# Half-chunk start, reordered loads and later filter stages in a fused layernorm, spectral filter and gated MLP kernel

## The chip, the cores and the metric

The kernel runs on one core of one Trainium2 chip. The metric is the device time of one execution in microseconds (us), lower is better. Times are medians of several executions; a "span" is the time from the first to the last instruction in the one execution that the trace shows, and it is about 2 us shorter than that execution's time. An execution that took over 1.5% more than the fastest of its kernel in its group counts as slow, and ratios leave it out.

Engine names in the profile: PE is TensorE's matmuls, PEld its weight loads, DVE is VectorE, ACT is ScalarE, POOL is GpSimd, SP is SyncE, which issues most DMAs.

## The reference

The input x has 2048 rows of 512 bf16 values. Two branches start from its layernorm, and their sum is added to x:

```
xn  = layernorm(x)                                   # over the 512 columns
A   = irfft2( rfft2(xn) * (w_r + i*w_i) )            # a filter over all rows and columns
B   = ( gelu(xn @ w_gate) * (xn @ w_up) ) @ w_down   # 512 -> 1792 -> 512
out = x + A + B
```

## The kernel before

One queue of instructions is written for each engine. TensorE runs its queue in order, so the writer decides by hand when each piece of the filter branch is put between the large matmuls of the MLP branch. The rows are cut in four chunks of 512 rows, each of four row tiles of 128. Where this text numbers rows, it means row tiles: rows 0 to 3 are chunk 0, rows 4 to 7 chunk 1. Matmuls write to the banks of PSUM, and the copy of a result out of a bank is called its eviction. For each chunk there are 14 blocks, each with a `gate` group and an `up` group (four matmuls of 512 columns each), and, one chunk later, four `down` groups. After each group stands a *hook*, a numbered place where other work may be put. There are 160 of them.

```
for b in range(4):                    # chunks
    for fc in range(NFC):             # 14 blocks
        gate(b, fc); hook(False)
        up(b, fc);   flush(); hook()
        if b > 0 and fc in (2, 5, 8, 11):
            down(b - 1, (fc - 2) // 3)      # 14 matmuls, three hooks inside
for jj in range(4):
    down(3, jj)
```

What hangs on the hooks, in the order of the data: normalisation of chunks 1 to 3 (`ln_stat`, `ln_aggr`, `ln_norm`), their transposes (`trans`), a butterfly of additions (`butter`, writes the "fold" tiles), the column transform (`unit_D`, 128-point units), the 64-point row-wise units (`unit_A`), a transposition through DRAM ("scr" written, "tv" read back), `unit_B` and the filter product, `unit_C`, a second trip through DRAM ("vp" written, the "vv" view of the arena read back), `unit_row`, `unit_E` and `unit_F`. In this document the first units after the tv reload (`unit_B`) are called column units, and A the row units. `unit_B` reads the whole of tv, so the first of them has to wait for the last reload.

```
for m in range(1, 4):
    a = 10 * (m - 1)
    ...  ln_stat at a .. a+3, ln_norm at a+6, a+7, trans at a+8, a+9, butter at a+10, a+11
for j in range(NJ):
    h = (4, 6, 8, 10, 12, 14, 17, 19, 22, 24, 27, 29, 32, 33, 34, 36)[j]
    at(h, (unit_D, j))
    if j % 2:
        at(h + 2, (unit_A, j - 1), (unit_A, j))
for i in range(0, 16, 2):
    at(47 + 3 * i, (unit_B, i), (unit_B, i + 1))
    at(52 + 3 * i, (unit_C, i), (unit_C, i + 1))
at(103, (unit_row,))
for j in range(NJ):
    at(104 + 3 * j, (unit_E, j))
    at(108 + 3 * j, (unit_F, j))
```

The start runs 24 dummy matmuls (`warm(24)`) while the first rows are loaded and normalised, then transposes the whole of chunk 0 and enters the loop:

```
warm(24)
for i in range(2): ln_stat(2*i); ln_stat(2*i + 1); ln_aggr(2*i, 2)
for i in range(2): ln_norm(2*i); ln_norm(2*i + 1)
for i in range(2):
    trans(0, (0, 1), (2*i, 2*i + 1), "dve")
    trans(0, (2, 3), (2*i, 2*i + 1), "act")
```

## Time and profile before

| | before |
|---|---|
| median of the executions of the first round | 206.12 us (205.89 to 207.45) |
| span in the trace (an execution of 207.09 us) | 205.1 us |
| TensorE busy | 190.8 us, 93% |
| first gate matmul, last eviction begins, end | 10.69, 201.37, 205.1 us |

The page's busy times, then two of its rows in 40 slices of 5.1 us each: how busy TensorE was in tenths, and the clock granted to it in tenths.

```profile
PE 190.8 (93%) x1131; PEld 93.2 (45%) x1145; DVE 112.1 (55%) x262; ACT 88.3 (43%) x157; POOL 25.9 (13%) x52
...
PE   7898989899999569999999999989999999999992
...
PEclk9999999999999957999999999999999999999999
```

TensorE is nearly always busy, and in one place, in slices 15 and 16, its clock was low. The next fence is TensorE's timeline there; columns: start, duration, engine, line of the kernel, operation, output and inputs, count, and in brackets how long the engine sat idle before and what ended it.

```profile
68.63 1.03 PE L589 MATMUL ps<-xnT,wu 128*128 128x512 f16 x4
73.51 1.07 PE L455 MATMUL ps<-tv,be 128*64 128x257 f16 x8 [3.85 <-DMA tv<-scr]
74.51 1.89 PE L576 MATMUL ps<-xnT,wg 128*128 128x512 f16 x4
76.19 1.91 PE L589 MATMUL ps<-xnT,wu 128*128 128x512 f16 x4
77.90 1.73 PE L576 MATMUL ps<-xnT,wg 128*128 128x512 f16 x4
79.47 1.03 PE L589 MATMUL ps<-xnT,wu 128*128 128x512 f16 x4
```

The first column unit (L455) waits 3.85 us for tv. Then the groups behind it take twice their time. A gate or up group starts 0.86 us after the one before it at full speed; here the starts are 1.7 us apart (74.51, 76.19, 77.90). The mean granted clock from 73.5 to 80 was 0.55. Asked in short stretches, the clock was at half from about 72.5 to 79.3.

TensorE's list of waits (total us, number of times, longest), the four lines that matter:

```profile
PE ps L455 <- DMA tv<-scr: 3.9, 1, 3.9
PE ps L366 <- DVE xn L356: 1.9, 5, 0.7
PE ps L406 <- DVE arena L392: 1.2, 2, 0.7
...
PE ps L501 <- DMA arena<-scr: 0.7, 1, 0.7
```

Besides tv there are waits for normalised rows (xn), for the butterfly (fold tiles, which lie in the arena) and, in front of `unit_row` (L501), for the second reload.

The start, timeline of all engines, chosen lines. L338 is the dummy matmuls, L356 normalises, L366 transposes, L344 takes statistics, L576 is gate.

```profile
1.19 6.84 PE L338 MATMUL ps<-dumm 128*128 128x512 f16 x24 [1.19 <-DVE dumm L309]
...
7.50 0.73 DVE L356 TENSOR_SCALAR xn<-x_sb,ag,rstd 128x512 f16<-128x512 bf16 x2
...
8.38 0.61 PE L366 MATMUL ps<-ident,xn 128*128 128x128 f16 x8 [0.35 <-DVE xn L356]
...
10.61 0.69 DVE L344 BATCH_NORM_STATS2 st<-x_sb 128x6 f32<-128x512 bf16 x1 [0.46 <-DMA x_sb<-in_A_x_dram]
...
10.69 1.02 PE L576 MATMUL ps<-xnT,wg 128*128 128x512 f16 x4 [0.78 <-ACT xnT L378]
...
14.14 1.03 PE L576 MATMUL ps<-xnT,wg 128*128 128x512 f16 x4
...
20.01 0.62 PE L366 MATMUL ps<-ident,xn 128*128 128x128 f16 x8 [0.73 <-DVE xn L356]
```

The 24 dummy matmuls end at 8.03. The first two rows are normalised at 8.23, the transposes follow, and gate begins at 10.69. The gate of the third block (which the change's half blocks lead up to) begins at 14.14.

The tail, same columns:

```profile
195.12 6.21 PE L602 MATMUL ps<-wd,hT 128*128 128x512 bf16 x27
...
201.37 0.69 DVE L615 TENSOR_TENSOR osb<-ps,x_sb 128x512 bf16<-128x512 f32 x1 [2.33 <-PE ps L602]
```

One eviction of 512 columns at 201.37, then the stores, and the end of the span at 205.1: 3.7 us from the start of that eviction.

### The profile page before, as it was taken

Reading aid. Unit: us, or ns where it says so; the run is one execution under the profiler, and the core shown is the slowest. Engines: PE = TensorE matmul, PEld = TensorE weight load, DVE = VectorE, ACT = ScalarE, POOL = GpSimd, SP = SyncE. Lnnn points to the kernel's source line nnn. Section 1 sums busy time; section 2 is a strip of 40 time slices with the busy share of each in tenths; the row PEclk is TensorE's granted clock in tenths of the full one; section 3 lists DMA queues with packets and bytes.
Section 4 is the critical chain, followed back from the end, with each engine's and each line's share of the span. In section 5 each row is a group of like instructions: output and inputs, shape, how many; then the busy total and the mean of one; then the engine's idle time right before and its main releaser. Section 6 shows DMA issues by size and latency. Waiting matters only on the chain.

```text
span 205.1 us, 3107 instructions
## 1 busy us (share of the span) xinstructions
PE 190.8 (93%) x1131; PEld 93.2 (45%) x1145; DVE 112.1 (55%) x262; ACT 88.3 (43%) x157; POOL 25.9 (13%) x52
## 2 busy tenths in 40 slices
PE   7898989899999569999999999989999999999992
PEld 3344544445544223444444444435555555555540
DVE  2897786978422233546773677233555454546341
ACT  2135565554553131563545534414636363635210
POOL 0201125031201202222310000000100001010000
PEclk9999999999999957999999999999999999999999
DMA  5999998626675601556654223230011111111102
GB/s 147 221 312 348 281 316 185 197 79 150 107 180 148 120 18 54 113 131 134 157 162 118 62 77 106 69 87 1 16 46 44 36 33 50 39 27 29 26 26 51
DMA packets 19007, 23.09 MB, mean 113 GB/s; under 512 B 2208, under 2 KB 16672, under 8 KB 18608
## 3 DMA queue, kind: packets, MB, share of 16 engines
q1 hardware_dynamic: 16512, 16.79, 30.4%
q0 software_dynamic: 1712, 5.32, 11.8%
q10 hardware_dynamic: 768, 0.79, 1.6%
q8 instruction: 9, 0.15, 0.3%
q14 instruction: 6, 0.05, 0.1%
HBM read 16.57 MB, written 6.31 MB: 112 GB/s over the span
## 4 chain that ended last, share of the span: by engine, by line
PE 73%; DMA 10%; DVE 10%; issue 2%; POOL 1%; ACT 1%; SPq 0%
PE ps L602 20%; PE ps L589 20%; PE ps L576 19%; DMA tv<-scr 3%; DVE hT L592 3%; DVE st L344 3%; PE ps L455 2%; PE ps L481 2%; DMA scr<-tt 2%; DMA scr<-vp 2%; PE ps L515 2%; DMA x_sb<-in_A_x_dram 2%; DMA arena<-scr 2%; DVE xn L356 2%; PE ps L366 1%
## 5 line engine op out<-in xcount | busy, mean ns | idle before, releaser
L592 DVE TENSOR_TENSOR hT<-ps,gl 128x512 bf16<-128x512 f32 x56 | 38.5, 690 | 41.8 <-PE ps L589 36.8
L576 PE MATMUL ps<-xnT,wg 128*128 128x512 f16 x224 | 59.2, 388 | 0.8 <-ACT xnT L378 0.8
L589 PE MATMUL ps<-xnT,wu 128*128 128x512 f16 x224 | 58.4, 384 | 0.0
L579 ACT ACTIVATE gl<-ps 128x512 bf16<-128x512 f32 x56 | 33.4, 597 | 48.1 <-PE ps L576 44.9
L602 PE MATMUL ps<-wd,hT 128*128 128x512 bf16 x210 | 49.8, 379 | 0.8 <-issue 0.2
L576 PEld LDWEIGHTS ps<-xnT,wg 128*128 128x128 bf16 x224 | 21.0, 99 | 24.5 <-issue 4.8
L602 PEld LDWEIGHTS ps<-wd,hT 128*128 128x128 bf16 x224 | 21.3, 98 | 23.2 <-issue 1.0
L589 PEld LDWEIGHTS ps<-xnT,wu 128*128 128x128 bf16 x224 | 21.3, 99 | 22.2 <-issue 2.6
L523 POOL COPY zt<-xn 1x128 bf16<-1x128 bf16 x16 | 4.5, 283 | 79.4 <-ACT zt L522 79.4
L615 DVE TENSOR_TENSOR x_sb<-ps,x_sb 128x512 bf16<-128x512 f32 x11 | 7.6, 690 | 12.0 <-PE ps L602 12.0
L522 ACT ACTIVATE zt<-ps 128x512 bf16<-128x512 f32 x16 | 9.5, 595 | 10.5 <-PE ps L515 10.5
L549 ACT ACTIVATE eo<-ps 128x512 bf16<-128x512 f32 x16 | 9.5, 595 | 9.4 <-PE ps L544 9.4
L487 ACT ACTIVATE vp<-ps 128x514 bf16<-128x514 f32 x16 | 8.7, 598 | 10.1 <-PE ps L481 10.1
L344 DVE BATCH_NORM_STATS2 st<-x_sb 128x6 f32<-128x512 bf16 x16 | 10.6, 685 | 3.6 <-DMA x_sb<-in_A_x_dram 3.6
L413 ACT ACTIVATE xs<-ps 128x512 f16<-128x512 f32 x16 | 9.5, 596 | 6.7 <-PE ps L409 6.6
L461 ACT ACTIVATE xc<-ps 128x514 f16<-128x514 f32 x16 | 8.7, 600 | 6.9 <-PE ps L455 6.9
L440 ACT ACTIVATE tt<-ps 128x514 f16<-128x514 f32 x16 | 8.7, 598 | 3.7 <-PE ps L434 3.1
L554 DVE TENSOR_TENSOR ys<-eo 128x256 bf16<-128x256 bf16 x16 | 4.6, 289 | 9.3 <-ACT eo L549 9.3
L455 PE MATMUL ps<-tv,be 128*64 128x257 f16 x64 | 5.5, 297 | 3.9 <-DMA tv<-scr 3.9
L467 DVE TENSOR_TENSOR m_0<-xc,Wr 128x514 bf16<-128x514 f16 x8 | 3.4, 430 | 10.3 <-ACT xc L461 10.3
L352 POOL TENSOR_TENSOR rstd<-vpe,mhalf 128x4 f32<-128x4 f32 (+1 forms) x5 | 4.6, 918 | 26.6 <-DVE vpe L351 26.6
L338 PE MATMUL ps<-dumm 128*128 128x512 f16 x24 | 6.8, 454 | 1.2 <-DVE dumm L309 1.2
(65 smaller groups left out, 167.2 us busy)
## 6 DMA issues: line engine op xcount, KB each, us to landing
scr<-tt SPq DMA_DIRECT2D x16, 128.5 KB
tv<-scr SPq DMA_DIRECT2D x16, 128.5 KB
scr<-vp SPq DMA_DIRECT2D x16, 128.5 KB
arena<-scr SPq DMA_DIRECT2D x16, 128.5 KB
out_dram<-osb SPq DMA_DIRECT2D x32, 64.0 KB
wg<-in_B_w_gate_dram SPq DMA_DIRECT2D x3, 512.0 KB, 11.2
wu<-in_B_w_up_dram SPq DMA_DIRECT2D x3, 512.0 KB, 13.0
x_sb<-in_A_x_dram SPq DMA_DIRECT2D x5, 256.0 KB, 11.4
```

The source lines that it names most:

```text
L344: op("dve", lambda e: e.bn_stats(st[:, j, :], x_sb[:, j, :]), r=[("x", j, 0), ("x", j, 1)], w=[("st", j)])
L413: op("act", lambda e: e.activation(x4[:].rearrange("p (a c r) -> p a c r", a=2, r=4), bank(bk).rearrange("p (a r c) -> p a c r", a=2, r=4) ...
L440: op("act", lambda e: e.activation(t4[:], pair(bk), ACT.Copy, scale=SC_A), r=[("ps", bk), ("ps", bk + 1)], w=[("tt", j % 4)])
L455: ins = e.matmul(bank(bk + ri)[64 * hh:64 * hh + 64, 0:257], be[:, 64 * ri:64 * ri + 64], tv[:, 16 * hh + h, :], start=True, stop=True, sk ...
L461: op("act", lambda e: e.activation(xc[s2][:, :, 0:KD], pair(bk), ACT.Copy, scale=SC_B), r=[("ps", bk), ("ps", bk + 1)], w=[("xc", s2)])
L522: op("act", lambda e: e.activation(z[:], bank(bk).rearrange("p (a c) -> p a c", a=4), ACT.Copy, scale=SC_E), r=[("ps", bk)], w=[zk])
L549: op("act", lambda e: e.activation(o2[:], bank(bk), ACT.Copy), r=[("ps", bk)], w=[ok])
L576: ins = e.matmul(bank(bg), wg_sb[:, dc, fc * P:(fc + 1) * P], xnT[:, dc, b * 512:(b + 1) * 512], start=(dc == 0), stop=(dc == 3))
L579: op("act", lambda e: e.activation(gl[k % 2][:], bank(bg), ACT.Gelu_apprx_tanh), r=[("ps", bg)], w=[("gl", k % 2)])
L589: ins = e.matmul(bank(bu), wu_sb[:, dc, fc * P:(fc + 1) * P], xnT[:, dc, b * 512:(b + 1) * 512], start=(dc == 0), stop=(dc == 3))
L592: op("dve", lambda e: e.tensor_tensor(hT[b % 2][:, fc, :], bank(bu), gl[k % 2][:], ALU.mult), r=[("ps", bu), ("gl", k % 2)], w=[("hT", b % ...
L602: ins = e.matmul(bank(bk), hT[b % 2][:, fc, jj * P:(jj + 1) * P], wd_sb[:, fc, :], start=(fc == 0), stop=(fc == NFC - 1))
```

## The change

Its intent: (1) begin the first two MLP blocks on the first half of chunk 0, before its second half is normalised; (2) load the weights of blocks 2 to 5 ahead of rows 4 to 7 and spread them over two queues; (3) give normalisation, transposes and butterfly more distance from one another; (4) put the column units far enough behind the row units that tv is back in time, and move the rest behind them; (5) halve the last down by columns, so that eviction and store of its first half overlap with the second. There is also a third gelu buffer, two z buffers fewer, and a better model of when PSUM banks come free. The core of the diff:

```diff
-        for b, eng in ((0, "sp"), (1, "act")):
-            load_x(4, 4, b, eng)
+        load_w(wg_sb, wgv, "wg", 2, 6, "act")
+        load_w(wu_sb, wuv, "wu", 2, 6, "sp")
+        load_x(4, 4, 0, "sp")
+        load_x(4, 4, 1, "sp")
         dma("sp", fd[:], c_fd.ap(), w=["fd"])
-        load_w(wg_sb, wgv, "wg", 2, 6, "sp")
-        load_w(wu_sb, wuv, "wu", 2, 6, "sp")
...   later loads reordered in the same way
-            a = 10 * (m - 1)
+            a = 9 * (m - 1) + 3
...   ln_norm at a+5 (was a+6), trans at a+9 (was a+8), butter at a+11 (was a+10),
...   butter of chunk 0 at 3 and 4 (was 0 and 1), late loads of the filter two hooks later
-            h = (4, 6, 8, 10, 12, 14, 17, 19, 22, 24, 27, 29, 32, 33, 34, 36)[j]
+            h = (9, 11, 13, 15, 17, 19, 21, 23, 26, 28, 30, 32, 35, 36, 37, 38)[j]
-            at(47 + 3 * i, (unit_B, i), (unit_B, i + 1))
-            at(52 + 3 * i, (unit_C, i), (unit_C, i + 1))
-        at(103, (unit_row,))
+            at(54 + 2.6 * i, (unit_B, i), (unit_B, i + 1))
+            at(61.8 + 2.6 * i, (unit_C, i), (unit_C, i + 1))
+        at(113, (unit_row,))
-            at(104 + 3 * j, (unit_E, j))
-            at(108 + 3 * j, (unit_F, j))
+            at(113 + 2.5 * j, (unit_E, j))
+            at(117 + 2.5 * j, (unit_F, j))
         warm(24)
...   stat 0, 1; aggr; stat 2; norm 0, 1; stat 3 in place of the old order
+        trans(0, (0, 1), (0, 1), "dve")
+        trans(0, (2, 3), (0, 1), "act")
...   aggr, norm 2, 3
+        gate(0, 0, (0, 1))
+        up(0, 0, (0, 1))
+        gate(0, 1, (0, 1))
+        trans(0, (0, 1), (2, 3), "dve")
+        trans(0, (2, 3), (2, 3), "act")
+        up(0, 1, (0, 1))
         for b in range(4):
             for fc in range(NFC):
+                jjs = (2, 3) if b == 0 and fc < 2 else (0, 1, 2, 3)
+        def last_down(bk):        # two halves of 256 columns, two banks
+            for c in range(2):
...             14 matmuls, one eviction of 256 columns, one store on SP and one on ACT
```

More of the change, by code (lines that the diff above doesn't have):

```diff
@@ L255, in bass_parallel_sum__spectral_gfnet__glu_gated_geglu__prompt_kernel @@
         vp = [sb("vp%d" % i, [P, 2, KD], BF16) for i in range(4)]
-        NZ = 6
+        NZ = 4
         zt = [sb("zt%d" % i, [P, 4, P], BF16) for i in range(NZ)]
@@ L259, in bass_parallel_sum__spectral_gfnet__glu_gated_geglu__prompt_kernel @@
         z256 = xn[:].rearrange("p a d -> p (a d)").bitcast(BF16)
-        gl = [sb("gl%d" % i, [P, 512], BF16) for i in range(2)]
+        gl = [sb("gl%d" % i, [P, 512], BF16) for i in range(3)]
         eo = [sb("eo%d" % i, [P, 512], BF16) for i in range(2)]
@@ L285, in bass_parallel_sum__spectral_gfnet__glu_gated_geglu__prompt_kernel, with take @@
         pt = [0.0]
+        act_t = [0.0]
         free = [0.0] * 8
-        def take(n, dur, hold):
+        def take(n, dur, hold=None):
             i = min(range(9 - n), key=lambda i: max(free[i:i + n]))
             pt[0] += dur
+            if hold is None:
+                act_t[0] = max(act_t[0], pt[0] + 0.25) + 0.62
+                end = act_t[0]
+            else:
+                end = pt[0] + hold
             for k in range(i, i + n):
-                free[k] = pt[0] + hold
+                free[k] = end
             return i
@@ L316, in bass_parallel_sum__spectral_gfnet__glu_gated_geglu__prompt_kernel @@
         load_w(wu_sb, wuv, "wu", 0, 2, "sp")
-        for b, eng in ((0, "sp"), (1, "act")):
-            load_x(4, 4, b, eng)
+        load_w(wg_sb, wgv, "wg", 2, 6, "act")
         op("act", lambda e: e.activation(warm_o[:], mhalf[:, 0:1], ACT.Gelu_apprx_tanh), r=["mhalf"], w=["warm_o"])
+        load_w(wu_sb, wuv, "wu", 2, 6, "sp")
+        load_x(4, 4, 0, "sp")
+        load_x(4, 4, 1, "sp")
         dma("sp", fd[:], c_fd.ap(), w=["fd"])
-        load_w(wg_sb, wgv, "wg", 2, 6, "sp")
-        load_w(wu_sb, wuv, "wu", 2, 6, "sp")
-        load_x(8, 4, 0, "sp")
-        load_x(8, 4, 1, "sp")
         dma("sp", am, c_am.ap().rearrange("p (j r c) -> p j r c", j=NJ, r=2), w=["am"])
@@ L327, in bass_parallel_sum__spectral_gfnet__glu_gated_geglu__prompt_kernel @@
         load_w(wu_sb, wuv, "wu", 6, 10, "sp")
+        load_x(8, 4, 0, "sp")
+        load_x(8, 4, 1, "sp")
+        load_w(wg_sb, wgv, "wg", 10, 14, "sp")
+        load_w(wu_sb, wuv, "wu", 10, 14, "sp")
         load_x(12, 4, 0, "sp")
         load_x(12, 4, 1, "sp")
-        load_w(wg_sb, wgv, "wg", 10, 14, "sp")
-        load_w(wu_sb, wuv, "wu", 10, 14, "sp")
         def warm(n):
@@ L397, in unit_D @@
         def unit_D(j):
-            bk = take(1, 0.33, 1.2)
+            bk = take(1, 0.33)
             m = j // 4
@@ L424, in unit_A @@
         def unit_A(j):
-            bk = take(2, 0.3, 1.6)
+            bk = take(2, 0.3)
             x4 = xs[j % 4]
@@ L448, in unit_B @@
         def unit_B(h):
-            bk = take(2, 0.3, 1.6)
+            bk = take(2, 0.3)
             def fn(e):
@@ L473, in unit_C @@
         def unit_C(h):
-            bk = take(2, 0.3, 1.6)
+            bk = take(2, 0.3)
             y = yy[h % 4]
@@ L498, in unit_row @@
         def unit_row():
-            bk = take(1, 0.1, 1.0)
+            bk = take(1, 0.1)
             op("pe", lambda e: e.matmul(bank(bk)[0:32, 0:64], vv[:, :, 256], EMs[:, 0:64], start=True, stop=True,
@@ L507, in unit_E @@
         def unit_E(j):
-            bk = take(1, 0.22, 1.2)
+            bk = take(1, 0.22)
             def fn(e):
@@ L536, in unit_F @@
         def unit_F(j):
-            bk = take(1, 0.44, 1.2)
+            bk = take(1, 0.44)
             def fn(e):
@@ L567, in bass_parallel_sum__spectral_gfnet__glu_gated_geglu__prompt_kernel, with gate @@
         gun = [0]
-        def gate(b, fc):
+        def gate(b, fc, jjs=(0, 1, 2, 3)):
             k = gun[0]
-            bg = take(1, 0.87, 1.2)
+            n = len(jjs) * P
+            c0 = b * 512 + jjs[0] * P
+            bg = take(1, 0.0017 * n)
             def fn(e):
@@ L575, in fn, with up @@
                 for dc in range(4):
-                    ins = e.matmul(bank(bg), wg_sb[:, dc, fc * P:(fc + 1) * P], xnT[:, dc, b * 512:(b + 1) * 512], start=(dc == 0), stop=(dc == 3))
+                    ins = e.matmul(bank(bg)[:, 0:n], wg_sb[:, dc, fc * P:(fc + 1) * P], xnT[:, dc, c0:c0 + n], start=(dc == 0), stop=(dc == 3))
                 return ins
-            op("pe", fn, r=[("wg", fc)] + xk(b), w=[("ps", bg)])
-            op("act", lambda e: e.activation(gl[k % 2][:], bank(bg), ACT.Gelu_apprx_tanh), r=[("ps", bg)], w=[("gl", k % 2)])
-        def up(b, fc):
+            op("pe", fn, r=[("wg", fc)] + [("xnT", b, dc, jj) for dc in range(4) for jj in jjs], w=[("ps", bg)])
+            op("act", lambda e: e.activation(gl[k % 3][:, 0:n], bank(bg)[:, 0:n], ACT.Gelu_apprx_tanh), r=[("ps", bg)], w=[("gl", k % 3)])
+        def up(b, fc, jjs=(0, 1, 2, 3), wait=False):
             k = gun[0]
             gun[0] += 1
-            bu = take(1, 0.87, 1.8)
+            n = len(jjs) * P
+            c0 = b * 512 + jjs[0] * P
+            bu = take(1, 0.0017 * n, 2.2)
             def fn(e):
@@ L588, in fn, with mult @@
                 for dc in range(4):
-                    ins = e.matmul(bank(bu), wu_sb[:, dc, fc * P:(fc + 1) * P], xnT[:, dc, b * 512:(b + 1) * 512], start=(dc == 0), stop=(dc == 3))
+                    ins = e.matmul(bank(bu)[:, 0:n], wu_sb[:, dc, fc * P:(fc + 1) * P], xnT[:, dc, c0:c0 + n], start=(dc == 0), stop=(dc == 3))
                 return ins
-            op("pe", fn, r=[("wu", fc)] + xk(b), w=[("ps", bu)])
-            op("dve", lambda e: e.tensor_tensor(hT[b % 2][:, fc, :], bank(bu), gl[k % 2][:], ALU.mult), r=[("ps", bu), ("gl", k % 2)], w=[("hT", b % 2, fc)])
+            op("pe", fn, r=[("wu", fc)] + [("xnT", b, dc, jj) for dc in range(4) for jj in jjs], w=[("ps", bu)])
+            h0 = jjs[0] * P
+            def mult():
+                op("dve", lambda e: e.tensor_tensor(hT[b % 2][:, fc, h0:h0 + n], bank(bu)[:, 0:n], gl[k % 3][:, 0:n], ALU.mult),
+                   r=[("ps", bu), ("gl", k % 3)], w=[("hT", b % 2, fc, jj) for jj in jjs])
+            if wait:
+                later.append(mult)
+            else:
+                mult()
+        def last_down(bk):
+            for c in range(2):
+                cs = slice(256 * c, 256 * c + 256)
+                bc = (bk + c) % 8
+                def fn(e, cs=cs, bc=bc):
+                    ins = None
+                    for fc in range(NFC):
+                        ins = e.matmul(bank(bc)[:, 0:256], hT[1][:, fc, 3 * P:4 * P], wd_sb[:, fc, cs], start=(fc == 0), stop=(fc == NFC - 1))
+                    return ins
+                op("pe", fn, r=[("wd", fc) for fc in range(NFC)] + [("hT", 1, fc, 3) for fc in range(NFC)], w=[("ps", bc)])
+                k = osb_n[0] % 3
+                osb_n[0] += 1
+                op("dve", lambda e, cs=cs, bc=bc, k=k: e.tensor_tensor(osb[k][:, cs], bank(bc)[:, 0:256], x_sb[:, NJ - 1, cs], ALU.add),
+                   r=[("ps", bc), ("acc", NJ - 1)], w=[("osb", k)])
+                for b, eng in ((0, "sp"), (1, "act")):
+                    dma(eng, ov[b, :, NJ - 1, cs], osb[k][64 * b:64 * b + 64, cs], r=[("osb", k)], w=[("out", NJ - 1, b, c)])
+            for _ in range(3):
+                hook()
         def down(b, jj):
@@ L604, in part @@
                 pt[0] += 0.217 * (f1 - f0)
-                op("pe", fn, r=[("wd", fc) for fc in range(f0, f1)] + [("hT", b % 2, fc) for fc in range(f0, f1)], w=[("ps", bk)])
+                op("pe", fn, r=[("wd", fc) for fc in range(f0, f1)] + [("hT", b % 2, fc, jj) for fc in range(f0, f1)], w=[("ps", bk)])
+            if j == NJ - 1:
+                return last_down(bk)
             part(0, 5)
@@ L645, in bass_parallel_sum__spectral_gfnet__glu_gated_geglu__prompt_kernel @@
         cmv = c_cm.ap().rearrange("p (j r c) -> p j r c", j=16, r=2)
-        for i, h0 in enumerate((26, 42, 52, 62)):
+        for i, h0 in enumerate((26, 44, 54, 64)):
             hs = slice(4 * i, 4 * i + 4)
@@ L659, in bass_parallel_sum__spectral_gfnet__glu_gated_geglu__prompt_kernel @@
             for i in range(4):
-                at(a + 6 + i // 2, (ln_norm, 4 * m + i))
-            at(a + 8, (trans, m, (0, 1), (0, 1, 2, 3)))
-            at(a + 9, (trans, m, (2, 3), (0, 1, 2, 3)))
-            at(a + 10, (butter, m, 0))
-            at(a + 11, (butter, m, 1))
-        at(0, (butter, 0, 0))
-        at(1, (butter, 0, 1))
+                at(a + 5 + i // 2, (ln_norm, 4 * m + i))
+            at(a + 9, (trans, m, (0, 1), (0, 1, 2, 3)))
+            at(a + 10, (trans, m, (2, 3), (0, 1, 2, 3)))
+            at(a + 11, (butter, m, 0))
+            at(a + 12, (butter, m, 1))
+        at(3, (butter, 0, 0))
+        at(4, (butter, 0, 1))
         for j in range(NJ):
-            h = (4, 6, 8, 10, 12, 14, 17, 19, 22, 24, 27, 29, 32, 33, 34, 36)[j]
+            h = (9, 11, 13, 15, 17, 19, 21, 23, 26, 28, 30, 32, 35, 36, 37, 38)[j]
             at(h, (unit_D, j))
@@ L672, in bass_parallel_sum__spectral_gfnet__glu_gated_geglu__prompt_kernel @@
         for i in range(0, 16, 2):
-            at(47 + 3 * i, (unit_B, i), (unit_B, i + 1))
-            at(52 + 3 * i, (unit_C, i), (unit_C, i + 1))
-        at(103, (unit_row,))
+            at(54 + 2.6 * i, (unit_B, i), (unit_B, i + 1))
+            at(61.8 + 2.6 * i, (unit_C, i), (unit_C, i + 1))
+        at(113, (unit_row,))
         for j in range(NJ):
-            at(104 + 3 * j, (unit_E, j))
-            at(108 + 3 * j, (unit_F, j))
+            at(113 + 2.5 * j, (unit_E, j))
+            at(117 + 2.5 * j, (unit_F, j))
         warm(24)
-        for i in range(2):
-            ln_stat(2 * i)
-            ln_stat(2 * i + 1)
-            ln_aggr(2 * i, 2)
-        for i in range(2):
-            ln_norm(2 * i)
-            ln_norm(2 * i + 1)
-        for i in range(2):
-            trans(0, (0, 1), (2 * i, 2 * i + 1), "dve")
-            trans(0, (2, 3), (2 * i, 2 * i + 1), "act")
+        ln_stat(0)
+        ln_stat(1)
+        ln_aggr(0, 2)
+        ln_stat(2)
+        ln_norm(0)
+        ln_norm(1)
+        ln_stat(3)
+        trans(0, (0, 1), (0, 1), "dve")
+        trans(0, (2, 3), (0, 1), "act")
+        ln_aggr(2, 2)
+        ln_norm(2)
+        ln_norm(3)
+        gate(0, 0, (0, 1))
[4 more added lines that the diff above has]
+        up(0, 1, (0, 1))
         for b in range(4):
             for fc in range(NFC):
-                gate(b, fc)
+                jjs = (2, 3) if b == 0 and fc < 2 else (0, 1, 2, 3)
+                gate(b, fc, jjs)
                 hook(False)
-                up(b, fc)
+                up(b, fc, jjs)
                 flush()
@@ L702, in bass_parallel_sum__spectral_gfnet__glu_gated_geglu__prompt_kernel @@
         assert not plan
-        pr.wait_all_dma("sp", [pr.writer[("out", j, b)] for j in range(NJ) for b in range(2)])
+        pr.wait_all_dma("sp", [ev for k, ev in pr.writer.items() if k[0] == "out"])
         with nc.Block() as block:
```

## The prediction

> **What bounds it now.** The page gives TensorE 190.8 of 205.1 us (93%); the chain of waits is almost all matmuls from the first gate matmul (10.69 us) to the last down matmul (ends 201.3). Time = start + TensorE's work + its holes + tail (3.8). A gate or up group takes 0.86 us at full clock, without gaps.
>
> Holes (timeline and waits of TensorE):
> - 3.85 us (69.6 to 73.5): the first column unit waits for the last "tv" reload, landed 12.0 us after the last row unit ended (61.35).
> - Then 73.5 to 80 ran at a granted clock of 0.55: the chain has 1.07, 1.82, 1.71, 1.53 us where such groups take 0.56, 0.97, 0.86, 0.86 elsewhere: 2.9 us. The Trainium skill, "TensorE: Matmul & The Clock Gate" (Part 1, the two states), says the clock halves after an idle window of about 3.4 us; this trace agrees (3.85 us idle, then 0.55).
> - 0.7 us at 138: unit_row waits for the second reload.
> - About 3.1 us in 19 to 48: transposes waiting for normalised rows (0.9, 0.4, 0.4), 128-point units for the butterfly (0.75, 0.7).
>
> **What the change does.**
> 1. Last row unit from hook 38 to 40, first column unit 47 to 54. Between them lie four gate/up blocks (1.73 each) and two downs (3.02 each): 13.0 us against the 12.0 needed. The late loads keep their distance. The wait goes or falls under 1 us, and the clock drop with it: 6.75 us.
> 2. Last C unit to unit_row: 9 hooks become 15: 0.7 us.
> 3. Normalisation to transpose gets 2 more hooks, butterfly to 128-point unit one more: I take 2.2 of 3.1 us.
> 4. Start: the first transposes could run at 7.6, but the warm-up matmuls end at 8.03, so the first half gate starts near 9.25, not 10.69. The second half of chunk 0 still passes through vector, pool, vector (0.45 + 0.8 + 0.75), transposes and copies, ready near 12.1. Eight half groups end near 13.8; the four full ones ended at 14.14. Gain 0.4 us, not 1.4.
> 5. Tail: the last eviction shrinks from 0.69 to about 0.4 us and its stores leave from two queues: 0.45 us. 256-column matmuls take 0.109 us each (F units), so halving is free.
> 6. Costs: x rows 4 to 7 land behind 1 MB of weights, I estimate at 13 to 14.5 us (GB/s row), so VectorE may stall 1 us, hidden by PSUM banks. VectorE, over 80% busy from 10 to 40 us, has less room. Later stages are tighter (5.2 hooks a pair, not 6): VectorE's 62% there becomes about 69%, no limit. The new bank model may add short waits. I allow 0.8 us.
>
> Sum: 6.75 + 0.7 + 2.2 + 0.4 + 0.45 - 0.8 = 9.7 us, all on the critical path, being TensorE's own holes, start or tail.
>
> **Predicted: 196.4 us, 194.0 to 200.0.** Faster by over 2%: 0.95; within 2%: 0.04; slower: 0.01.
>
> **What would show it.** Step 1: no TensorE wait over 1 us on tv, no dip in the clock row. Step 2: no wait of unit_row. Step 3: waits on xn and fold below 1 us in sum. Step 4: first gate matmul near 9.3 us, the third block's gate near 13.8. Step 5: last matmul to end about 3.3 us, not 3.8. TensorE's busy sum falls by about 3 us, its idle by about 6.
>
> **What would make it wrong.** The tv reload may take over 12 us; over about 3.4 us of idle would bring the clock drop back (then 200 to 203). VectorE, in order, may hold up banks in the first 40 us (1 to 3 us). Bank waits in the filter stage.

## The result

The changed kernel took 197.34 us in the median of four executions (196.42 to 198.12), against 206.47 us (205.89 to 207.45) for the kernel before. The ratio is 0.955, with a 95% interval of 0.949 to 0.961. All ratios here are the mean time of one kernel's fast runs over that of the other's of the same rounds, so they are not quite the ratio of the medians. The time forecast was 196.4 us, with a range of 194.0 to 200.0.

The trace was taken from the slowest of the four executions (198.12 us, span 196.1 us). The page's lines that answer to those of before:

```profile
PE 188.6 (96%) x1161; PEld 95.8 (49%) x1175; DVE 112.0 (57%) x265; ACT 88.9 (45%) x159; POOL 26.2 (13%) x52
...
PE   7989899999999999999999999999999999999993
...
PEclk9999999999999999999999999999999999999999
```

The dip in the clock row is gone. TensorE's idle time in the span fell from 14.3 us (205.1 less 190.8) to 7.5, and its busy time by 2.2 us, although the dummy matmuls took 1.2 us longer in this execution. TensorE's timeline at the tv reload (L441 is the last row unit, L462 the first column unit):

```profile
62.04 0.27 PE L441 MATMUL ps<-xs,arena 64*128 64x255 f16 x2
...
75.30 0.63 PE L462 MATMUL ps<-tv,be 128*64 128x257 f16 x8
75.87 1.04 PE L585 MATMUL ps<-xnT,wg 128*128 128x512 f16 x4
```

The row units end at 62.31 and the column units begin at 75.30. That is 13.0 us of other work, and nothing is waited for. TensorE's list of waits, the lines that matter:

```profile
PE ps L373 <- DVE xn L363: 1.2, 1, 1.2
...
PE ps L585 <- ACT xnT L385: 1.1, 2, 0.8
```

No wait for tv, for the arena or at `unit_row` is left. One wait for xn remains, of 1.2 us. The start (L345 dummy matmuls, L363 normalisation, L373 transposes, L585 gate, L351 statistics):

```profile
1.19 8.01 PE L345 MATMUL ps<-dumm 128*128 128x512 f16 x24 [1.19 <-DVE dumm L316]
...
6.61 0.73 DVE L363 TENSOR_SCALAR xn<-x_sb,ag,rstd 128x512 f16<-128x512 bf16 x2 [0.20 <-POOL rstd L359]
...
9.04 0.61 PE L373 MATMUL ps<-ident,xn 128*128 128x128 f16 x8
...
10.43 0.60 PE L585 MATMUL ps<-xnT,wg 128*128 128x256 f16 x4 [0.78 <-ACT xnT L385]
...
15.00 1.03 PE L585 MATMUL ps<-xnT,wg 128*128 128x512 f16 x4
...
15.90 0.69 DVE L351 BATCH_NORM_STATS2 st<-x_sb 128x6 f32<-128x512 bf16 x1 [0.22 <-DMA x_sb<-in_A_x_dram]
...
24.82 0.62 PE L373 MATMUL ps<-ident,xn 128*128 128x128 f16 x8 [1.23 <-DVE xn L363]
```

Here the surprise is. Rows 0 and 1 are normalised at 7.34, but the dummy matmuls take 8.01 us in this execution, not 6.84, and the transposes are behind them in TensorE's queue. The first half gate begins at 10.43. The third block's gate begins at 15.00, which is 0.86 us *later* than before. The statistics of chunk 1 begin at 15.90, and VectorE waited for their rows. The first transpose of chunk 1 waits 1.23 us, until 24.82.

The tail (L622 is the halved last down, L627 its evictions):

```profile
189.91 3.22 PE L622 MATMUL ps<-wd,hT 128*128 128x256 bf16 x28
...
191.64 0.42 DVE L627 TENSOR_TENSOR osb<-ps,x_sb 128x256 bf16<-128x256 f32 x1 [0.84 <-PE ps L622]
...
193.17 0.42 DVE L627 TENSOR_TENSOR osb<-ps,x_sb 128x256 bf16<-128x256 f32 x1 [1.10 <-PE ps L622]
```

From the start of the last eviction to the end it is now 2.9 us, 0.8 less. The two spans balance: the third gate is 0.86 us later; from there to the last eviction it is 178.17 us (193.17 less 15.00) and was 187.23 (201.37 less 14.14), 9.06 less; the tail is 0.80 less. Together that is 9.0 us. Of the 9.06, the wait for tv is 3.85, the low clock 2.9 and `unit_row` 0.7. The remaining 1.6 is what is left over: the listed waits for xn and the butterfly after the first gate fell from 2.4 to 1.2 us, and the rest was not taken apart.

### The profile page after: what moved, and what is told of

Its sections match the earlier page's. It is cut to its first block, busy times and chain, and to the rows that moved or that the text cites. A ratio compares the mean times of both kernels' runs of the same rounds, so it can differ in the third digit from the quotient of the medians.

```text
span 196.1 us, 3164 instructions
## 1 busy us (share of the span) xinstructions
PE 188.6 (96%) x1161; PEld 95.8 (49%) x1175; DVE 112.0 (57%) x265; ACT 88.9 (45%) x159; POOL 26.2 (13%) x52
## 4 chain that ended last, share of the span: by engine, by line
PE 83%; DMA 6%; DVE 5%; SPq 2%; issue 1%; ACT 1%; POOL 1%; DVEq 0%
PE ps L642 23%; PE ps L585 22%; PE ps L600 21%; DMA x_sb<-in_A_x_dram 6%; PE ps L462 2%; PE ps L488 2%; SPq L304 2%; PE ps L522 2%; PE ps L622 2%; PE ps L373 2%; PE ps L437 1%; DVE st L351 1%; PE ps L441 1%; PE ps L549 1%; PE ps L550 1%
## 5 line engine op out<-in xcount | busy, mean ns | idle before, releaser
L606 DVE TENSOR_TENSOR hT<-ps,gl 128x512 bf16<-128x512 f32 (+1 forms) x58 | 38.9, 670 | 37.8 <-PE ps L600 36.7
L585 PE MATMUL ps<-xnT,wg 128*128 128x512 f16 (+1 forms) x232 | 57.9, 372 | 1.1 <-ACT xnT L385 1.1
L600 PE MATMUL ps<-xnT,wu 128*128 128x512 f16 (+1 forms) x232 | 57.9, 372 | 0.0
L588 ACT ACTIVATE gl<-ps 128x512 bf16<-128x512 f32 (+1 forms) x58 | 33.8, 582 | 43.3 <-PE ps L585 41.3
L642 PE MATMUL ps<-wd,hT 128*128 128x512 bf16 x196 | 47.2, 379 | 1.0 <-issue 0.2
L585 PEld LDWEIGHTS ps<-xnT,wg 128*128 128x128 bf16 x232 | 21.5, 98 | 22.3 <-issue 2.6
L642 PEld LDWEIGHTS ps<-wd,hT 128*128 128x128 bf16 x210 | 19.9, 98 | 21.1 <-issue 0.8
L657 DVE TENSOR_TENSOR x_sb<-ps,x_sb 128x512 bf16<-128x512 f32 x12 | 8.3, 690 | 16.4 <-PE ps L642 16.4
L351 DVE BATCH_NORM_STATS2 st<-x_sb 128x6 f32<-128x512 bf16 x16 | 10.8, 685 | 3.1 <-DMA x_sb<-in_A_x_dram 3.1
L345 PE MATMUL ps<-dumm 128*128 128x512 f16 x24 | 8.0, 512 | 1.2 <-DVE dumm L316 1.2
L363 DVE TENSOR_SCALAR xn<-x_sb,ag,rstd 128x512 f16<-128x512 bf16 x16 | 6.2, 432 | 2.6 <-POOL rstd L359 2.6
L308 POOL DMA_DIRECT2D Wr<-in_A_w_r_dram x8 | 5.0, 624 | 19.2 <-PE ps L642 13.4
```

The lines of the kernel that those rows point to most:

```text
L351: op("dve", lambda e: e.bn_stats(st[:, j, :], x_sb[:, j, :]), r=[("x", j, 0), ("x", j, 1)], w=[("st", j)])
L585: ins = e.matmul(bank(bg)[:, 0:n], wg_sb[:, dc, fc * P:(fc + 1) * P], xnT[:, dc, c0:c0 + n], start=(dc == 0), stop=(dc == 3))
L588: op("act", lambda e: e.activation(gl[k % 3][:, 0:n], bank(bg)[:, 0:n], ACT.Gelu_apprx_tanh), r=[("ps", bg)], w=[("gl", k % 3)])
L600: ins = e.matmul(bank(bu)[:, 0:n], wu_sb[:, dc, fc * P:(fc + 1) * P], xnT[:, dc, c0:c0 + n], start=(dc == 0), stop=(dc == 3))
L606: op("dve", lambda e: e.tensor_tensor(hT[b % 2][:, fc, h0:h0 + n], bank(bu)[:, 0:n], gl[k % 3][:, 0:n], ALU.mult), r=[("ps", bu), ("gl", k ...
L642: ins = e.matmul(bank(bk), hT[b % 2][:, fc, jj * P:(jj + 1) * P], wd_sb[:, fc, :], start=(fc == 0), stop=(fc == NFC - 1))
```

## The experiments

Twelve runs were made in three groups (e9 is the changed kernel again). Each group ran on one chip with its own runs of the kernel before (fast-run means 206.9, 206.0 and 206.1 us). All gave correct results. On the chip of e5 to e8 one execution of before took only 204.35 us, at a mean clock of 0.998, and five of its eleven count as slow beside it; with all executions counted, the means of before are 207.2 and 206.9 us on the first two chips.

### e1: the late stages alone

Theory: the gain lies in the wait for tv and what it triggers. Rival: it came from start and loads, or the waits only move.

```diff
 kernel before:
-            at(47 + 3 * i, ...B)      at(52 + 3 * i, ...C)      at(103, row)  104 + 3 * j, 108 + 3 * j
+            at(54 + 2.6 * i, ...B)    at(61.8 + 2.6 * i, ...C)  at(113, row)  113 + 2.5 * j, 117 + 2.5 * j
```

> The kernel before with only the later hooks of the column, multiply, row-of-256 and 32-point stages taken from the change; its start, loads, early hooks and last down stay. My theory: the wait for the tv reload (3.85 us), the clock drop after it (2.9 us) and the wait of unit_row (0.7 us) go: about 199.0 us, clock 1.00 in every slice. Rival: those waits only move, or the gain came from the loads and the start: over 202.5 us.

Measured: 199.85 us (199.61 to 200.40), ratio 0.967 (0.963 to 0.971), clock 1.00 in all slices of the trace (means of 0.996 to 1.000 in the four executions), no wait for tv or at `unit_row`. Against 206.9 us this is 7.0 us from five lines of hook numbers, three quarters of the whole gain. The rival fell.

### e2: fill the wait, but keep it

This separates the low clock from the wait itself.

```diff
 kernel before:
+        plan[47].insert(0, (fill, 16))    # 16 matmuls on zeros, 512 columns, own bank, ahead of unit_B(0)
```

> The kernel before with 16 dummy matmuls of 512 columns (about 3.5 us) put in front of the first column unit, so the tv reload is still waited for but TensorE is busy in most of the wait. My theory (the clock drop is caused by the idle stretch): the first column unit still starts near 73.5, but the four groups behind it take 0.56, 0.97, 0.86, 0.86 us: 2.9 us less, about 203.4 us, clock 1.00. Rival (the clock drops for another reason, at that work or that time): no change, 206.3 us, clock about 0.55 in 73 to 80.

Measured: 205.40 us, but in two groups: 204.35 and 204.39, and 206.41 and 206.76; ratio 0.991 (0.986 to 0.997). The granted clock, as a mean over the span, was 0.998 to 1.000 in all four, where the fast runs of before had 0.983 to 0.991. The trace is of the 206.76 us execution; its TensorE timeline (L349 dummies, L465 column unit, L586 gate, L599 up):

```profile
70.50 3.62 PE L349 MATMUL ps<-dumm 128*128 128x512 f16 x16
75.30 0.64 PE L465 MATMUL ps<-tv,be 128*64 128x257 f16 x8 [1.18 <-DMA tv<-scr]
75.86 1.04 PE L586 MATMUL ps<-xnT,wg 128*128 128x512 f16 x4
76.74 1.03 PE L599 MATMUL ps<-xnT,wu 128*128 128x512 f16 x4
```

TensorE still waits 1.18 us for tv, and every group behind runs at full speed (starts 0.86 us apart). So the idle stretch caused the low clock; the position and the kind of work did not. The time fell less than expected in this execution: the row units ended 1.0 us later than in the trace of before (62.35, was 61.35), tv took 12.7 us from there and not 12.0, and the second reload was waited for by 1.37 us, not 0.7. How long a reload takes differs by over 1 us between executions (e11's took 13.4, see there); why is not settled. The lower pair of times is 2.5 us under the mean of before. The 2.9 us of the theory is also the long case: a mean clock of 0.983, as in the trace of before, stands for some 7 us at half clock, and 0.991 for some 3.7 (estimates, (1 less mean clock) times span over 0.5). Only 10 of the 33 executions of before in the three groups had 0.983, and all but one of the others 0.988 to 0.992.

### e3, e4, e9, e11: the start, half or whole, with 24 or 16 dummy matmuls

The trace of after says that the half start made the third gate later, not earlier. My theory: the half start can pay only when the dummy matmuls are out of its way.

```diff
 e3 (changed kernel, whole start):
-                jjs = (2, 3) if b == 0 and fc < 2 else (0, 1, 2, 3)
+                jjs = (0, 1, 2, 3)          # and the start sequence of before
 e4 (changed kernel, half start):
-        warm(24)
+        warm(16)
 e11: both edits.   e9: the changed kernel once more, unaltered.
```

> The changed kernel with its first two blocks on the whole of chunk 0 again, and the statistics, normalisations and transposes in the order of before; loads, hooks and last down stay. If the half start gains 0.4 us as I predicted: 197.7 us. Rival, from the trace of after (its third block's gate began at 15.00, before it was 14.14): the half start loses up to 0.9 us, so this gives 196.4 to 196.9, with the third block's gate near 14.1.

> The changed kernel with 16 warm-up matmuls, not 24. If the first transposes wait for the end of the warm-up (9.04 in the trace of after, rows normalised at 7.34): they start near 7.4, the first half gate near 8.8, the third block's gate near 13.6 at full clock, and the time falls by 0.8 to 1.4 us. Rival: the shorter warm-up leaves the clock low, so that the first gates run at half speed and the time stays or rises by up to 1 us; or the start is bound by the loads, and nothing changes.

> The changed kernel once more, unaltered, for a second trace and for times in the same rounds as the three runs beside it. If its time is set by the warm-up (whose 24 matmuls took between 6.8 and 8.1 us in the traces so far): the third block's gate begins 5.8 us after the end of the warm-up (9.20 to 15.00 in the first trace), as long as the warm-up ends after about 7.3; times spread over more than 1 us, median 197.3. Rival: the third gate's time does not follow the warm-up's end.

> e3 (the changed kernel with the whole-chunk start) with 16 warm-up matmuls, the fourth corner of half or whole start by 24 or 16. If the half start pays only once the warm-up is out of its way: the whole start, held by VectorE's normalisation to 8.3 and not by the warm-up, gains nothing from 16: 197.2 us, third block's gate at 14.1, against 196.5 for the half start with 16. Rival: the gain of e4 came from the shorter warm-up alone: about 196.5 here too.

Times are medians with the lowest and highest execution; ratios are against before in the same rounds. The last two columns are from the traces, each of one execution: that of e4 is its fastest, that of after its slowest, the others lie between.

| start | dummies | us | ratio | third gate | first transpose of chunk 1 |
|---|---|---|---|---|---|
| half (after) | 24 | 197.34 (196.42 to 198.12) | 0.955 | 15.00 | 24.82 |
| half (e9) | 24 | 197.44 (196.53 to 198.74) | 0.958 | 14.12 | 24.37 |
| whole (e3) | 24 | 197.27 (197.13 to 197.51) | 0.954 | 14.14 | 23.96 |
| half (e4) | 16 | 196.60 (196.08 to 198.29) | 0.951 | 13.43 | 22.80 |
| whole (e11) | 16 | 197.45 (196.97 to 199.22) | 0.960 | 13.96 | 23.78 |

With 24 dummies, half and whole start are the same within the noise: the half start, for which the change was partly written, brought nothing. With 16, the half start is about 0.7 us better than e3 in the median of the same rounds (ratios 0.951 and 0.954; the intervals overlap, so the trace decides). The shorter warm-up alone (e11) brings next to nothing: in its trace the third gate and the transpose come 0.18 us earlier than in e3. The rival for e11 fell. So did the rival for e4 that a short warm-up leaves the clock low: its first half gate and half up start 0.43 us apart, half of the 0.86 us of a whole group. But e11's trace, taken in the middle of its times, has a wait for tv again:

```profile
75.02 0.64 PE L462 MATMUL ps<-tv,be 128*64 128x257 f16 x8 [0.69 <-DMA tv<-scr]
```

From the end of the row units (61.27) this reload took 13.4 us, more than the 13.0 us of work that the change puts between. The new distance is just enough, not safe. Two of e11's six executions, 199.04 and 199.22 us, had a mean clock of 0.991 where the others had 0.999 to 1.000; a longer wait and a dip there would fit, but no trace of them was taken.

The timeline of e4:

```profile
1.20 6.02 PE L345 MATMUL ps<-dumm 128*128 128x512 f16 x16 [1.20 <-DVE dumm L316]
...
7.48 0.61 PE L373 MATMUL ps<-ident,xn 128*128 128x128 f16 x8 [0.26 <-DVE xn L363]
...
8.86 0.60 PE L585 MATMUL ps<-xnT,wg 128*128 128x256 f16 x4 [0.78 <-ACT xnT L385]
...
13.43 1.03 PE L585 MATMUL ps<-xnT,wg 128*128 128x512 f16 x4
...
14.02 0.68 DVE L351 BATCH_NORM_STATS2 st<-x_sb 128x6 f32<-128x512 bf16 x1
...
22.80 0.62 PE L373 MATMUL ps<-ident,xn 128*128 128x128 f16 x8 [0.78 <-DVE xn L363]
```

and of e9, the changed kernel again:

```profile
1.19 7.13 PE L345 MATMUL ps<-dumm 128*128 128x512 f16 x24 [1.19 <-DVE dumm L316]
...
8.16 0.61 PE L373 MATMUL ps<-ident,xn 128*128 128x128 f16 x8
...
14.12 1.03 PE L585 MATMUL ps<-xnT,wg 128*128 128x512 f16 x4
...
15.59 0.69 DVE L351 BATCH_NORM_STATS2 st<-x_sb 128x6 f32<-128x512 bf16 x1 [0.80 <-DMA x_sb<-in_A_x_dram]
...
24.37 0.62 PE L373 MATMUL ps<-ident,xn 128*128 128x128 f16 x8 [1.66 <-DVE xn L363]
```

In e9 the warm-up ends at 8.32 and the third gate begins 5.80 us later, exactly as in the first trace (9.20 and 15.00), as the expectation said. So the dummies do delay the start. But e9 reached the third gate 0.88 us earlier than the first trace and the transpose of chunk 1 only 0.45 us earlier. The gap in front of that transpose grew from 1.23 to 1.66 us. The reason is in VectorE's line: its first statistics of chunk 1 begin at 15.59 there and at 15.90 in the first trace. In all five rows of the table the transpose comes 8.8 to 9.0 us after the beginning of those statistics (15.90, 15.59, 14.95, 14.02 and 14.77), whenever the third gate was. And from that transpose to the end of the span it is 171.3 us in after, e3 and e4, 171.4 in e9, and 172.1 in e11 with its wait for tv. The chain of after that ended last (`--critical`) runs the same way: the load of rows 4 to 7 until 15.8, VectorE's statistics, normalisation, and the transpose at 24.82. The start is therefore worth what it does for the statistics of chunk 1. In after and e9 these waited 0.2 and 0.8 us for rows 4 to 7, which the change loads behind the weights. In e3 and e4 VectorE did not wait for them at all. The rows landed by 14.0 in e4 and at about 15.6 in e9, from the same load order; why the landing differs by over 1.5 us between executions stays open.

### e5: the old load order, with the short warm-up

```diff
 e4, with the load list of before (rows 4 to 7 ahead of the weights of blocks 2 to 5)
```

> The changed kernel with 16 warm-up matmuls (as e4) and the order of the loads of before: x rows 4 to 7 ahead of the weights of blocks 2 to 5. If the reordering is what lets the early third block start: its gate (13.43 in e4) or its up now waits for its weights, 1 to 2 us are lost, about 198 us. Rival: the weights arrive in time in either order (before had its third gate at 14.14 without a wait), rows 4 to 7 come earlier, and the time stays at 196.6 or falls by up to 0.5 us.

Measured: 196.34 us (196.06 to 197.54), ratio 0.949 (0.944 to 0.953), no worse than e4, which ran on another chip. The 198 us of the theory did not come. But in the traced execution, the slowest, TensorE waited three times for `up` weights, 2.0 us in all. Only one of these waits is that of the theory, at block 2:

```profile
15.76 1.04 PE L600 MATMUL ps<-xnT,wu 128*128 128x512 f16 x4 [0.64 <-DMA wu<-in_B_w_up_dram]
```

The other two, 0.60 us at block 0 and 0.74 at block 6, have their like in the trace of e10 (0.41 and 0.53), which has the new order, so the old order alone does not explain them. In the same trace of e5 no wait for xn is left, as the rival says. For this start I can't call either order better.

### e12: old early hooks, new load order

```diff
 e3, with the hooks of before for normalisation, transposes, butterfly, unit_D and unit_A
```

> e3 with the early hooks of before but the load order of the change: rows 4 to 7 (15.8 us in the trace of after) behind the weights, while their statistics stand at hook 0 of VectorE's queue. If loads and hooks had to move together: VectorE waits some 3 us from about 12.7 for the rows, the transposes of chunk 1 come late, TensorE idles there, and the time is 1 to 3 us over e8: 200 to 202 us. Rival: the PSUM banks and the slack hide it, 199.2.

Measured: 202.25, 202.91 and 203.25 us in the fast runs, and 205.53 in a slow one; ratio 0.984. That is more than the 200 to 202 us expected. VectorE's first statistics of chunk 1 and the first 128-point unit on TensorE, from the timeline of all engines:

```profile
14.21 0.69 DVE L351 BATCH_NORM_STATS2 st<-x_sb 128x6 f32<-128x512 bf16 x1 [4.05 <-DMA x_sb<-in_A_x_dram]
...
18.11 0.22 PE L413 MATMUL ps<-fd,arena 128*128 128x128 f16 x1 [2.93 <-DVE arena L399]
```

VectorE sat idle for 4.05 us because the statistics stood at hook 0 of its queue and the rows came only at 14.2. The butterfly stands behind them, and TensorE idled 2.93 us for it. With the load order also of before (e8, next) the time is 199.2. So the two parts have to move together: the new order of loads needs the later hooks.

### e8: old early hooks and old load order

```diff
 e3, with the early hooks of before and the load list of before
```

> e3 with the early hooks (normalisation, transposes, butterfly, 128-point and row units) and the order of the loads of before; the late stages and the tail are those of the change. My theory: the holes in front of transposes and 128-point units come back (2.4 us in e1 against 1.2 in e3): 1.2 to 1.6 us slower, 198.6 to 198.9 us. Rival: those holes are matched by later starts of the units, so the early hooks are worth nothing: 197.3.

Measured: 199.17 us (198.75 to 200.30), ratio 0.962, against 0.954 for e3: 0.8 points, about 1.7 us; the traces' spans differ by 1.7 us too (197.0 and 195.3). The waits on xn and the fold tiles in the trace are 3.1 us in all (0.75 of it in the start, before the first gate), and 1.2 in e3.

### e7: the last down in one piece

```diff
 e3, without the call of last_down
```

> e3 (the changed kernel with the whole-chunk start, which is the steadiest) with the last down in one piece of 512 columns and its two stores on one queue. My theory from the tails of the two traces (3.8 us from the last matmul to the end before, 3.0 after): 0.8 us slower, 198.0 us against 197.27. My prediction said 0.45 us. Rival: the halving costs on TensorE what it gives back: 197.3.

Measured: 198.06 us (197.82 to 198.69), ratio 0.956; e3 has 197.27 us and 0.954. The medians differ by 0.8 us, the traces' spans by 0.7 (196.0 and 195.3), the ratios by only 0.2 points, about 0.45 us, with intervals that overlap. The two ran on different chips, and on e7's five executions of before were left out as slow; with all of them counted the ratios differ by 0.5 points, about 1.1 us. The spans, which have the same third gate (14.14) and the same first transpose of chunk 1 (23.96), are the cleanest of these measures.

### e6 and e10: one hook more for chunk 1

These try to remove what is left of the wait for xn.

```diff
 e6 = e4, with
-            at(a + 9, (trans, 1, ...))   at(a + 10, ...)  at(a + 11, (butter, 1, 0)) at(a + 12, (butter, 1, 1))
+            at(a + 10, (trans, 1, ...))  at(a + 11, ...)  at(a + 12, (butter, 1, 0)) at(a + 13, (butter, 1, 1))
-            h = (9, 11, 13, 15, 17, 19, ...
+            h = (9, 11, 13, 15, 18, 19, ...
 e10 = e6, with  h = (9, 11, 13, 15, 19, 20, ...
```

> The changed kernel with 16 warm-up matmuls (as e4), and the transposes and butterfly of chunk 1, and its first 128-point unit, one hook later. In e4 TensorE waits 0.78 us at 22 for the normalised rows of chunk 1, after the 1.23 us of the trace of after. If the wait is one of order alone: it goes, about 195.9 us. Rival: VectorE, which is busy without a break from 14 to 24 us, is late anyway, and the wait moves to the 128-point unit: 196.6.

> e6 with the first two 128-point units of chunk 1 another hook later (18, 19 to 19, 20), because e6 waits 0.5 us for the butterfly there. If that wait is one of order: it goes, 195.5 us. Rival: it stays or moves, 196.0. In any case faster than the changed kernel by 1 us or more.

Measured: e6 196.02 us (195.97 to 197.67), ratio 0.948; e10 196.56 us (194.98 to 196.95), ratio 0.952. In e6's trace no wait for the rows of chunk 1 is left, and 0.48 us before its 128-point unit instead, where e4 had 0.78 us before the transpose. In e10's trace, its slowest execution, that wait is gone, but TensorE waited 0.9 us for `up` weights and 0.7 for xn (0.3 of it in the start), and VectorE 1.09 us for rows 4 to 7. The two cannot be told apart. e10 ran in the same rounds as the changed kernel (e9): the ratio of their means is 196.24 / 197.51 = 0.994, so the short warm-up and the shifted hooks beat the change by about 1.3 us there, and e6 is of the same size. Its expected 195.5 us was not reached. In e10's trace the waits left are for early loads and what follows from them; that these limit the other executions too is not shown.

## Why the prediction was right, and where it was not

- **The sum.** 9.7 us were predicted and 9.1 measured (206.47 less 197.34). The mechanism, TensorE's own holes, was right; the parts were partly mis-sized. Taken apart by experiments they give 7.0 (e1) + 1.7 (e8) + 0.7 (e7) + 0 for the start (e3), 9.4 us in all, which leaves about nothing for the gelu and z buffers and the bank model, which were not tried apart. That the total came so close is in part luck: steps 1 to 4 brought about 1.3 us less than forecast, step 5 some 0.3 more, and of the 0.8 us allowed for costs hardly any shows as a separate cost.
- **Step 1, tv wait and clock: right.** 6.75 us plus 0.7 for step 2; e1 has both alone at 7.0 us. The other work between row and column units lasted 13.0 us, as worked out from hooks. The need was not a fixed 12.0 us: the reload took 12.7 in e2 and 13.4 in e11, where 0.69 us was waited for again. The Trainium skill, "TensorE: Matmul & The Clock Gate" (Part 1), has the two clock states and the idle window of about 3.4 us; e2 shows that the idle stretch was the cause here: 3.85 us idle gave a mean clock of 0.55 after it, and a wait for the same reload with dummies in most of it gave full speed. In the trace of before the clock fell at about 72.5, 2.9 us after the last matmul ended (69.66), so the figure measured here is shorter than the page's. In e12's traced execution 2.93 us of idle gave no dip (mean clock 1.00); its three other executions, untraced, had 0.983 to 0.992.
- **Step 2, `unit_row`: right.** The wait is gone.
- **Step 3, early holes: mis-sized.** "I take 2.2 of 3.1 us": the 3.1 was too high to begin with, as the list of waits before has 2.4 us outside the start; after it has 1.2 left, not under 1. By trace about 1.6 us was gained between the third gate and the end; e8 gives about 1.7 us for the early hooks with their loads.
- **Step 4, start: wrong.** "Gain 0.4 us": the gain was zero by e3 and e9, and minus 0.86 us in the first trace. I took the warm-up's end (8.03) from one trace as fixed. It takes 6.84 to 8.12 us for the same 24 matmuls from one execution to another. The skill's same part calls the cold start "run-variable" because the window is free-running; its Part 2 says that matmuls stay in program order, which is why the transposes stand behind the dummies. I also judged the start by the third gate, but the time is carried on by VectorE's statistics of chunk 1 and the transposes that follow them.
- **Step 5, tail: right in kind, too small.** 0.45 us predicted, 0.8 measured by the traces, 0.7 by the spans of e7 and e3. The last eviction shrank from 0.69 to 0.42 us as assumed. The rest, about 0.5 us, came after it: 3.04 us from the end of the last eviction to the end before, 2.51 after. The skill, "DMA: Bandwidth & Descriptors" (Anatomy of one DMA), puts a fixed cost of about 2.0 us on a DMA (its figure is for DMAs issued by GpSimd, while these stores are issued by SyncE and ScalarE); both tails here lie above it. How much of the 0.5 us is the second queue and how much the smaller store was not tried apart.
- **Step 6, costs: small, but not hidden.** Rows 4 to 7 came at 15.6 to 15.9 us in after and e9, not at 13 to 14.5, and VectorE waited 0.2 to 0.8 us for them. "Hidden by PSUM banks" was wrong: the transpose of chunk 1 follows the statistics by 8.8 to 9.0 us, so their delay is passed on. TensorE has two waits of 0.16 us in the filter stage, one put down to VectorE, and no others there, so the new bank order added next to nothing. VectorE's share from 75 to 128 us is 64% (33.79 of 52.70 us), under the 69% expected.

## What to carry to other kernels

A wait on the busiest engine that is long enough to lower its clock can cost well over its own length (here 6.75 us for 3.85 in the traced execution), so look for it first, and remove it by distance: count the work between producer and consumer against the measured round trip. A part that starts earlier gains only as much as the next fixed point of the pipeline moves; compare the start of that next point (here, the transpose of chunk 1) between traces, not the start of the part. Dummy warm-up work stands in the same queue as real work, and its length varies from run to run; give it no more than fits in front of the data.

## What the Trainium skill lacked or had wrong

- "TensorE: Matmul & The Clock Gate", Part 1, says the ramp is run-variable and worth under 1% of a span. Here it is 0.8 to 1.5% (an estimate: 24 matmuls at the later 0.22 us would take 5.2 us), though much of it runs while the first rows load. The page lacks what that means for dummy matmuls ahead of real ones: 24 of them took 6.84 to 8.12 us and 16 took 5.15 to 6.23 us, and the first half gate moved from 9.55 to 10.43 us with them.
- The same part gives at least one window, about 3.4 us, of sustained work until the clock is back, and names no upper end. After the dip here the work was slow from 73.51 to about 79.3, 5.8 us, and the clock was low for 6.8 us in all. On the way down the clock row fell 2.9 us after the (modelled) end of the last matmul, not 3.4.
- No page says how far the landing of one load order varies: rows 4 to 7 were there by 14.0 us in e4, and only at 15.6 to 15.9 us in the traces of after, e9 and e10, which have the same order of loads.
- The profile's clock row shows 1.00 while the dummies run, although the 24 took 0.29 to 0.34 us each and the same size takes 0.22 later. Part 1 warns in general that the trace's clock-gate events can be unreliable; no page says that a clock row can miss a cold start.
